# Packed attention and a channel mixer on one core: two sweeps over halves of w2's rows, in one manual order with planned side steps

## The chip, the cores and the metric

The kernel runs on one core of one Trainium2 chip. A core has TensorE (PE, matrix products into PSUM), VectorE (DVE), ScalarE (ACT), GpSimd (POOL) and SyncE (SP, which here issues every DMA). Engines run their own instructions in program order and wait for each other by semaphores. The metric is the device time of one execution in microseconds (us); lower is better.

## The reference, cut to what matters

```python
# q, k, v: (8, 8, 576, 64); p: (8, 8, 32, 64); U: (576, 32); V: (32, 576)
# w_ch1: (512, 2048); w_ch2: (2048, 512); the last four arrive as float64
def sm_attn(qq, kk, vv):
    s = scale * np.matmul(qq, kk.transpose(0, 1, 3, 2))
    s = s - np.max(s, axis=-1, keepdims=True)
    a = np.exp(s)
    a = a / (np.sum(a, axis=-1, keepdims=True) + 1e-09)
    return np.matmul(a, vv)
p_packed = sm_attn(p, k, v)
out = sm_attn(q, p_packed, p_packed)
x = out.transpose(0, 2, 1, 3).reshape(8, 576, 512)
h = x.transpose(0, 2, 1) @ U @ V
u = x + h.transpose(0, 2, 1)
ch = np.maximum(u @ w_ch1, 0.0) @ w_ch2
return (u + ch).astype(np.float32)
```

For each of 8 batches, 32 packed tokens per head attend to all 576 tokens, and all tokens then attend to the 32 packed ones. A low-rank mixing over the tokens and a two-layer perceptron follow. Since `out` is a product of attention weights (576 x 32 per head) with `p_packed`, the kernel never forms it: it multiplies `p_packed` into w1 ahead of time (the fold, giving 256 rows by 2048 columns for each batch) and mixes the attention weights instead of the tokens.

## The kernel before, in words

Products in the perceptron use three matmuls each (`mm3`): both operands are split into a rounded part (h) and a rest (l). The float64 weights are read as pairs of words and turned to float32 in chunks of 128 x 512 by `float32_of` (one ACT and four DVE instructions, L67 to L71), and then split (L123 ACT, L124 POOL).

**First stage** (L482 on, ordered by the scheduler). Over 16 units, half a batch's heads each: loads of k and v; a DVE transpose of k (L101); scores against a block diagonal of p (`a_scores`, L325, plain fp32); softmax; transposes of the weights on PE (`a_turn`, L345); packed tokens (`a_pack`, L361). Beside it all 16 chunks of w1 are converted and split, U and V are prepared (`prepare_uv`), and the folds for batches 0 to 3 are multiplied (`fold`, L384) and stored to DRAM (`wsr`). `attention(0)` runs here too.

**Main loop** (L695 on, in manual order). For each batch and each of 16 blocks kt of 128 hidden channels: `gemm1(kt)` (12 matmuls into `h_ps`, in two halves of 256 and 320 tokens), then ACT's Relu into `hh` (L641) and DVE's rest `hl` (L643), with the last 64 tokens kept in `hjh` and `hjl`; `gemm2(kt - 1)` adds 12 matmuls into four PSUM banks `o`, one for each 128 tokens. For each second batch `joint` (L671) makes the product of the kept tokens of two batches. `add_u` adds the residual. The folded weights are loaded by `load_wt` from DRAM and split by `split_wt` (L455 ACT, L456 POOL), a piece for two kt.

Side work stands at fixed places of that loop, one step each: `attention(b + 2)` as 16 closures (DVE transpose of q, scores with split operands, softmax on ACT, DVE and POOL, transposes `t_ps` L228, `m_ps`, `v_ps`), the conversion of w2's 16 tiles in batch 0, and the fold for batches 4 to 7, for which w1 is loaded and converted again (`later`, L554).

Of the kernel before, what the change touches and what calls it, by code (L numbers as in the profile page):

```python
# [15 lines left out]
DRAM = bass.MemoryType.DRAM  # L16


@with_exitstack
def packed_attention_mixer_kernel(  # L20
# [22 lines left out]

    nc = tc.nc
# [6 lines left out]
    NB = S // 32  # L51
    SM = 512
    NK = DF // P
    NU = 2 * B
    QW = 256
    scale = 1.0 / float(D) ** 0.5
    HALF = ((0, 256), (256, 320))
# [4 lines left out]

    def float32_of(x, t, raw):


        low, high = raw[:, :, 0], raw[:, :, 1]
        nc.scalar.activation(t, high.bitcast(F32), AF.Abs)  # L67
        nc.vector.tensor_single_scalar(t, t, LEAST, op=ALU.max)  # L68
        nc.vector.tensor_scalar(x, t.bitcast(I32), 3, 0x3FFFFFF8, op0=ALU.logical_shift_left, op1=ALU.bitwise_and)  # L69
        nc.vector.scalar_tensor_tensor(x, high, -0x40000000, x, op0=ALU.bitwise_and, op1=ALU.bitwise_or)  # L70
        nc.vector.scalar_tensor_tensor(x, low, 29, x, op0=ALU.logical_shift_right, op1=ALU.bitwise_or)  # L71
        return x.bitcast(F32)
# [10 lines left out]
    psT = ctx.enter_context(tc.tile_pool(name="psT", bufs=2, space=PSUM))  # L83

# [3 lines left out]
    bdq = const.tile([P, 4, P], F32, name="bdq")  # L88
    nc.gpsimd.memset(bdq, 0.0)

    wsr = [dram.tile([2 * H * NP, DF], F32, name=f"wsr{r}", tag=f"wsr{r}") for r in range(2)]
    wsc = {b: dram.tile([H * NP, DF], F32, name=f"wsc{b}", tag=f"wsc{b}") for b in range(B // 2, B)}


    def load_nat(pool, bufs, src, b, g):
        nat = pool.tile([P, NB * D], F32, name="nat", bufs=bufs)
        nc.sync.dma_start(out=nat, in_=src[b, 4 * g:4 * g + 4].rearrange("h (i c) d -> (h i) (c d)", c=NB))
        return nat

    def transposed(t, nat):  # L100
        nc.vector.transpose(  # L101
            t.rearrange("p h (i c) -> p c h i", c=NB),
            nat.rearrange("p (c h l) -> p c h l", h=2, l=32),
        )
        return t


    def weight_tiles(name):
        return [
            tuple(pipe.tile([P, DF], F32R, name=f"{name}{x}{i}", tag=f"w{x}{i}") for x in "hl") for i in range(4)  # L110
        ]

    def conv_tile(dtype):
        return pipe.tile([P, DM], dtype, name="os", bufs=3)
# [4 lines left out]
    def fold_tile(dtype):  # L119
        return pipe.tile([P, 512], dtype, name="fold", bufs=6)  # L120

    def split(x, hi, lo):
        nc.scalar.copy(hi, x)  # L123
        nc.gpsimd.tensor_tensor(lo, x, hi.bitcast(F32), op=ALU.subtract)  # L124


    uh = const.tile([P, 5, 4, R], F32R, name="uh")
    ul = const.tile([P, 5, 4, R], F32R, name="ul")
    vs = const.tile([P, S], F32R, name="vs")

    def load_uv(pool):
        bits = pool.tile([P, NB * D], F32, name="nat", bufs=3)
        ub = bits[:, :10 * R].bitcast(I32)
        nc.gpsimd.memset(ub[64:, 8 * R:], 0)
        nc.sync.dma_start(out=ub[:, :8 * R].rearrange("p (k r) -> p k r", k=4),
                          in_=U[:SM].rearrange("(k p) r -> p k r", p=P))
        nc.sync.dma_start(out=ub[:64, 8 * R:], in_=U[SM:])
        vbits = pool.tile([P, NB * D], F32, name="nat", bufs=3).bitcast(I32)
        for a in range(4):
            nc.sync.dma_start(out=vbits[32 * a:32 * a + 32], in_=V)  # L140
        return ub, vbits

    def prepare_uv(ub, vbits):
        ux = float32_of(conv_tile(I32)[:, :5 * R], conv_tile(F32)[:, :5 * R], ub.rearrange("p (x t) -> p x t", t=2))
        for (n, ks) in ((P, slice(0, 4)), (64, slice(4, 5))):
            nk = ks.stop - ks.start
            src = ux.rearrange("p (k r) -> p k r", k=5)[:n, ks].unsqueeze(2).to_broadcast([n, nk, 4, R])
            nc.vector.tensor_copy(uh[:n, ks], src)
            nc.vector.tensor_tensor(ul[:n, ks], src, uh[:n, ks].bitcast(F32), op=ALU.subtract)
        vb = vbits.rearrange("p (x t) -> p x t", t=2)  # L150
        for c0 in (0, S // 2):
            cs = slice(c0, c0 + S // 2)
            vx = float32_of(conv_tile(I32)[:, :S // 2], conv_tile(F32)[:, :S // 2], vb[:, cs])
            nc.vector.tensor_copy(vs[:, cs], vx)
            for a in (2, 3):
                as_ = slice(32 * a, 32 * a + 32)
                nc.vector.tensor_tensor(vs[as_, cs], vx[as_], vs[as_, cs].bitcast(F32), op=ALU.subtract)


    def attention(b, res):  # L160

        st = {}

        def load(g):
            st["nat", g] = load_nat(pipe, 1, q, b, g)

        def blocks():
# [18 lines left out]
        def scores(g, hf):  # L186
            hi, lo = st["q", g]
            bqh, bql = st["bq"]
            if hf == 0:
                st["e", g] = pipe.tile([P, NB, 32], F32, name="e", bufs=1)  # L190
# [215 lines left out]
    def convert_w1(c):  # L406
        x = float32_of(conv_tile(I32), conv_tile(F32), wbits.pop(c))
        if c + 2 < 16:
            wbits[c + 2] = load_w1(c + 2)
# [378 lines left out]
```

## Time and profile before

| what | value |
|---|---|
| median of the runs | 877.01 us (876.28 to 878.86, three runs) |
| the profiled execution's own time | 877.77 us |
| its span, first to last instruction | 876.0 us |
| TensorE's mean granted clock | 0.987 |
| DMA, mean over the span | 112 GB/s, 98.55 MB |
| POOL busy | 258.6 us (30%) |

The page sums each engine's busy time and follows back the chain of work that ended last. The views by window give busy times for a stretch. The timeline gives starts and lengths; lengths of matmuls are modelled and overlap, so the distance between starts is the rate. A row of a group reads: line, engine, operation, out<-in, shapes, count, then busy us and mean ns, then the engine's idle time ahead of these instructions and who ended it.

### The profile page before, as it was taken

Reading aid. Unit: us, or ns where it says so; the run is one execution under the profiler, and the core shown is the slowest. Engines: PE = TensorE matmul, PEld = TensorE weight load, DVE = VectorE, ACT = ScalarE, POOL = GpSimd, SP = SyncE. Lnnn points to the kernel's source line nnn. Section 1 sums busy time; section 2 is a strip of 40 time slices with the busy share of each in tenths; the row PEclk is TensorE's granted clock in tenths of the full one; section 3 lists DMA queues with packets and bytes.
Section 4 is the critical chain, followed back from the end, with each engine's and each line's share of the span. In section 5 each row is a group of like instructions: output and inputs, shape, how many; then the busy total and the mean of one; then the engine's idle time right before and its main releaser. Section 6 shows DMA issues by size and latency. Waiting matters only on the chain.

```text
span 876.0 us, 12670 instructions
## 1 busy us (share of the span) xinstructions
PE 827.1 (94%) x4480; PEld 708.5 (81%) x4480; DVE 518.6 (59%) x1042; ACT 374.6 (43%) x960; POOL 258.6 (30%) x230
## 2 busy tenths in 40 slices
PE   4779898889999999999999999999999999999997
PEld 2556576677879888888888888988888889889886
DVE  7999986789767875577675443443543524432220
ACT  2557676534444554456554332233332322333220
POOL 3302353545443213132323232323241313221110
PEclk9989999999999999999999999999999999999999
DMA  9769775823333444344453103010301120002001
GB/s 316 237 208 331 213 225 207 256 87 126 128 100 108 120 148 124 97 121 121 124 172 85 52 19 112 26 56 13 112 25 64 62 62 25 25 13 96 25 1 60
DMA packets 59998, 98.55 MB, mean 112 GB/s; under 512 B 12192, under 2 KB 36768, under 8 KB 59936
## 3 DMA queue, kind: packets, MB, share of 16 engines
q1 hardware_dynamic: 59936, 97.75, 35.9%
q8 instruction: 35, 0.57, 0.3%
q14 instruction: 27, 0.22, 0.1%
HBM read 71.52 MB, written 26.21 MB: 112 GB/s over the span
## 4 chain that ended last, share of the span: by engine, by line
PE 72%; DVE 18%; DMA 4%; issue 3%; ACT 3%; SPq 0%; DVEq 0%; ACTq 0%
PE o L78 15%; PE o L76 14%; PE o L77 14%; PE h_ps L76 7%; PE h_ps L77 7%; PE h_ps L78 7%; DVE kT L101 4%; DVE os L70 2%; DVE os L69 2%; DVE os L71 2%; PE w_ps L595 2%; DVE natT L101 2%; DVE os L68 2%; DMA bits<-in_moe_w_ch_dram 1%; PE t_ps L228 1%
## 5 line engine op out<-in xcount | busy, mean ns | idle before, releaser
L643 DVE SCALAR_TENSOR_TENSOR hl<-h_ps,hh 128x256 fp32r<-128x256 f32 x256 | 104.1, 418 | 180.2 <-ACT hh L641 145.0
L78 PE MATMUL o<-w2h,hl 128*128 128x512 f32 x512 | 201.8, 394 | 0.0
L76 PE MATMUL o<-w2h,hh 128*128 128x512 f32 x512 | 200.9, 392 | 0.0
L77 PE MATMUL o<-w2l,hh 128*128 128x512 f32 x512 | 200.4, 391 | 0.0
L641 ACT ACTIVATE hh<-h_ps 128x256 fp32r<-128x256 f32 x256 | 96.1, 383 | 235.0 <-PE h_ps L78 232.0
L76 PE MATMUL h_ps<-ah,fold 128*128 128x256 f32 x496 | 149.7, 302 | 7.5 <-DVE hl L643 7.1
L456 POOL TENSOR_TENSOR fold<-fold 128x512 fp32r<-128x512 f32 x62 | 81.4, 1313 | 230.7 <-ACT fold L455 225.3
L77 PE MATMUL h_ps<-al,fold 128*128 128x256 f32 x496 | 146.5, 295 | 0.0
L78 PE MATMUL h_ps<-ah,fold 128*128 128x256 f32 x496 | 146.0, 294 | 0.0
L78 PEld LDWEIGHTS o<-w2h,hl 128*128 128x128 f32 x512 | 96.1, 188 | 21.3
L77 PEld LDWEIGHTS o<-w2l,hh 128*128 128x128 f32 x512 | 96.4, 188 | 17.6
L76 PEld LDWEIGHTS o<-w2h,hh 128*128 128x128 f32 x512 | 96.3, 188 | 16.7
L76 PEld LDWEIGHTS h_ps<-ah,fold 128*128 128x128 f32 x496 | 93.7, 189 | 14.7 <-DVE hl L643 11.5
L77 PEld LDWEIGHTS h_ps<-al,fold 128*128 128x128 f32 x496 | 93.9, 189 | 2.1
L78 PEld LDWEIGHTS h_ps<-ah,fold 128*128 128x128 f32 x496 | 93.8, 189 | 0.0
L184 POOL TENSOR_TENSOR nlo<-natT,nhi 128x576 fp32r<-128x576 f32 x32 | 46.0, 1453 | 114.8 <-ACT nhi L183 114.8
L68 DVE TENSOR_SCALAR os<-os 128x512 f32<-128x512 f32 (+2 forms) x51 | 39.5, 775 | 35.4 <-ACT os L67 35.4
L325 PE MATMUL s_ps<-kT,bdp 128*128 128x288 f32 x128 | 39.7, 460 | 9.5 <-DVE bdp L316 9.3
L183 ACT CAST nhi<-natT 128x576 fp32r<-128x576 f32 x32 | 20.7, 675 | 56.3 <-DVE natT L101 53.2
L101 DVE STREAM_TRANSPOSE kT<-nat 128x1152 f32<-128x1152 f32 x16 | 37.3, 2330 | 5.8 <-DMA nat<-in_k_dram 5.7
L325 PEld LDWEIGHTS s_ps<-kT,bdp 128*128 128x128 f32 x128 | 26.4, 215 | 17.6 <-issue 9.3
L124 POOL TENSOR_TENSOR w1l<-os,w1h 128x512 fp32r<-128x512 f32 x16 | 21.2, 1328 | 62.3 <-ACT w1h L123 62.3
(145 smaller groups left out, 1419.7 us busy)
## 6 DMA issues: line engine op xcount, KB each, us to landing
bits<-in_moe_w_ch_dram SPq DMA_DIRECT2D x48, 512.0 KB, 4.3
nat<-in_k_dram SPq DMA_DIRECT2D x16, 576.0 KB, 4.9
nat<-in_q_dram SPq DMA_DIRECT2D x16, 576.0 KB, 4.5
vt<-in_v_dram SPq DMA_DIRECT2D x16, 512.0 KB, 5.5
wsr<-fold SPq DMA_DIRECT2D x32, 256.0 KB, 3.7
out_dram<-bits SPq DMA_DIRECT2D x16, 512.0 KB, 3.0
wsc<-bits SPq DMA_DIRECT2D x64, 128.0 KB, 2.2
fold<-wsc SPq DMA_DIRECT2D x32, 256.0 KB, 2.8
```

Of the source, the lines that this page charges most:

```text
L68: nc.vector.tensor_single_scalar(t, t, LEAST, op=ALU.max)
L76: nc.tensor.matmul(ps, lhsT=lh, rhs=rh, start=start, stop=False)
L77: nc.tensor.matmul(ps, lhsT=lh, rhs=rl, start=False, stop=False)
L78: nc.tensor.matmul(ps, lhsT=ll, rhs=rh, start=False, stop=stop)
L101: nc.vector.transpose(t.rearrange("p h (i c) -> p c h i", c=NB), nat.rearrange("p (c h l) -> p c h l", h=2, l=32),)
L124: nc.gpsimd.tensor_tensor(lo, x, hi.bitcast(F32), op=ALU.subtract)
L183: nc.scalar.copy(hi[:, dh], t)
L184: nc.gpsimd.tensor_tensor(lo[:, dh], t, hi[:, dh].bitcast(F32), op=ALU.subtract)
L325: nc.tensor.matmul(s_ps[:, hf, :288], lhsT=bdp[b % 2][:, 2 * g + dh], rhs=kT[:, dh, 288 * hf:288 * hf + 288], start=dh == 0, stop=dh == 1)
L456: nc.gpsimd.tensor_tensor(lo, raw, hi.bitcast(F32), op=ALU.subtract)
L641: nc.scalar.activation(hi, src, AF.Relu)
L643: nc.vector.scalar_tensor_tensor(lo, src, 0.0, hi.bitcast(F32), op0=ALU.max, op1=ALU.subtract)
```

## The change

The main loop becomes two sweeps: kt 0 to 7 for all eight batches, then kt 8 to 15. The first sweep's sums go to DRAM (`sums`, `sumj`) and are added when the second sweep's are stored; the split tokens go to DRAM as well (`asp`) and are loaded again (`reload_a`). Only half of w1 (two quarters of its columns at a time) and half of w2 are held; w2's later half is converted in the first sweep, kept in DRAM (`w2d`) and reloaded between the sweeps. w1 is converted once.

There is no first stage by itself. The whole program is in manual order. Packs, attention, folds and conversions are generators; each yields after a step and tells the PE time, the engine times, the PSUM banks and the buffers of its next one. A planner, `Chains`, keeps a clock of each engine and, after each half of `gemm1` and each tile of `gemm2`, places the steps that are ready by it, earliest due first. `until` lets its clock run until named steps are done. The loop starts after `until("attention0", "fold0_0", "w2_0")`.

Further: k and q are turned by PE transposes (`turn`: nine of 128 x 128 for each unit, with ACT and DVE copies out of PSUM) instead of DVE's L101; scores are eight fp32 matmuls with 64 rows and 32 columns for each unit, for q unsplit; the packed tokens are 20 matmuls 32 columns wide. The halves of `gemm1` are 288 tokens each, and 32 kept tokens come from each half. `mixing` takes 10 matmuls for 15. V is converted once on 128 partitions, stored to DRAM (`vd`) and loaded back four times.

```diff
+class Chains:
+    def ready(self, name):
+        c = self.left[name]
+        return (c["at"] <= self.now
+                and (c["due"] <= self.horizon or max(self.free["DVE"], self.free["ACT"]) <= self.now)
+                and all(n in self.flags or n in self.done and self.done[n] <= self.now for n in c["after"])
+                and all(t <= self.now for t in self.banks[:c["need"]])
+                and all(self.resources[r] >= c["take"].count(r) for r in c["take"]))
...
+    def place(self, pe=0.0, ops=()):
+        self.spend(pe, ops)
+        banks = went = 0
+        for _ in range(4):
+            names = [n for n in self.left if (banks == 0 or self.left[n]["need"] == 0) and self.ready(n)]
+            if not names:
+                break
+            name = min(names, key=lambda n: self.left[n]["due"])
+            banks += self.left[name]["need"]
+            self.go(name)
+            went += 1
+        return went
+    def until(self, *names):
+        while not all(n in self.flags or n in self.done and self.done[n] <= self.now for n in names):
+            if not self.place():
+                self.now += 0.1
...
+    side = Chains(6, xt=NX, xT=2, e=3, eT=2, pT=1, aT0=1, aT1=1)
+    side.slow = 1.7
...
+        nc.sync.dma_start(out=vd, in_=vx)
+        v4 = sA.tile([P, S], F32, name="v4")
         for a in range(4):
-            nc.sync.dma_start(out=vbits[32 * a:32 * a + 32], in_=V)
+            nc.sync.dma_start(out=v4[32 * a:32 * a + 32], in_=vd.rearrange("(r a) x -> r (a x)", a=P // R))
...
+    def turn(x, t, **then):
+        pairs = x.rearrange("p a x -> p (a x)")
+        for h2 in range(2):
+            t_ps = bank()
+            for a in range(4):
+                c = 4 * h2 + a
+                nc.tensor.transpose(t_ps[:, P * a:P * a + P], pairs[:, P * c:P * c + P], ident)
+            nc.scalar.copy(t[:, 2 * h2:2 * h2 + 2, HT:HS], t_ps.rearrange("p (h x) -> p h x", h=2))
+            yield step(0.45, ("ACT", 0.59), need=1, wait=False)
...
+    def scores(lT, t, g):
+        ss = [bank() for _ in range(2)]
+        for h in range(4):
+            hs = slice(32 * h, 32 * h + 32)
+            for r in range(2):
+                rs = slice(64 * r, 64 * r + 64)
+                nc.tensor.matmul(ss[r][hs, :HS], lhsT=lT[rs, g, hs], rhs=t[rs, h, HT * (1 - r):HT * (1 - r) + HS], start=True, stop=True)
+        return ss
...
+        yield step(0.75, ("DVE", 1.2), ("ACT", 1.4), need=1, take=("eT",))
...
+        for kk in range(5):
+            rows = P if kk < 4 else 64
             for h in range(4):
                 hs = slice(32 * h, 32 * h + 32)
+                rhs = vk[:, kk, h] if kk < 4 else vx[:rows, 4, D * h:D * h + D]
+                nc.tensor.matmul(p_ps[hs, :D], lhsT=eT[:rows, kk, hs], rhs=rhs, start=kk == 0, stop=kk == 4)
...
+        yield step(1.1, ("ACT", 0.35), need=1)
...
+    def fold(r, parts, fresh=(0, 1)):
...
+            for pr in range(4):
+                w_ps = bank()
+                mm3(w_ps, (lwh[:, pr], lwl[:, pr]), w1_slices(pr, c), True, True)
+                st = out_tile()
                 nc.scalar.copy(st, w_ps)
+                for b2 in batches:
+                    nc.sync.dma_start(out=wsb[2 * r + b2, c][64 * pr:64 * pr + 64], in_=st[64 * b2:64 * b2 + 64])
...
+    side.until("attention0", "fold0_0", "w2_0")
+    for i in range(2):
+        load_wt(i)
+        split_wt(i)
...
+            for hf in range(2):
+                n0, n = HS * hf, HS
...
+                side.place(0.8, [("ACT", 0.58), ("DVE", 0.6)])
...
+                mm3(self.o[t], (hh[:, ts_], hl[:, ts_]), w2t[kt], kt == self.kts[0], kt == self.kts[-1])
+                side.place(0.7)
+        def store(self):
+            for t in range(4):
+                os_ = out_tile()
...
+                if self.sw == 1:
+                    nc.vector.tensor_tensor(os_, self.o[t], self.part[:, t], op=ALU.add)
...
+    for sw in range(2):
...
+        for b in range(B):
+            if sw == 0 and b > 0:
+                side.until(f"attention{b}")
+            cur = Batch(sw, b)
...
+                if (sw, b) == (0, 0) and j == 2:
+                    side.until("fold0_1")
+                    load_wt(2)
+                if sw == 0 and b % 2 == 1 and j == 4 and b + 1 < B:
+                    side.until(f"fold{(b + 1) // 2}")
...
+                cur.gemm1(kt)
...
+                if j > 0:
+                    if (sw, b) == (0, 0):
+                        side.until(f"w2_{kt - 1}")
+                    cur.gemm2(kt - 1)
...
+                        if sw == 1 and b == 0:
+                            for k2 in range(NKS, NK):
+                                reload_w2(k2)
...
+                side.place()
```

More of the change, by code (lines that the diff above doesn't have):

```diff
@@ L19, in packed_attention_mixer_kernel, with step @@
+def step(pe, *ops, need=0, take=(), due=None, wait=True, after=()):
+    return pe, ops, need, take, due, wait, after
 @with_exitstack
@@ L100, in transposed @@
[L100 to L114, printed above, removed]
+    ppT = {}
+    ppTd = [dram.tile([P, 2 * P], F32, name=f"ppTd{b}", tag=f"ppTd{b}") for b in range(B)]
```

1062 lines of the change are left out of this document (532 added, 530 removed).

## The prediction

> **What bounds the kernel now.** I read the page first, then the windows, then TensorE's timeline. The page says what the end hangs on:
>
> ```profile
> span 876.0 us, 12670 instructions
> PE 827.1 (94%) x4480; PEld 708.5 (81%) x4480; DVE 518.6 (59%) x1042; ACT 374.6 (43%) x960; POOL 258.6 (30%) x230
> PE 72%; DVE 18%; DMA 4%; issue 3%; ACT 3%; SPq 0%; DVEq 0%; ACTq 0%
> ```
>
> TensorE (PE) holds 72% of the chain that ended last, and VectorE (DVE) 18%. The windows (columns: stretch, length, then busy us and instructions of PE, PEld, DVE, ACT, POOL; clock; DMA share; GB/s) show that these are two different kernels, one after the other:
>
> ```profile
> 0.00:160.40 160.40, 127.08 (x529) 92.79 (x530) 140.59 (x247) 94.43 (x235) 56.12 (x64) 0.95 0.79 250
> 160.40:876.00 715.60, 699.98 (x3952) 615.72 (x3950) 378.06 (x795) 280.16 (x726) 202.45 (x166) 1.00 0.27 82
> 25.00:125.00 100.00, 85.56 (x361) 63.28 (x360) 95.88 (x175) 63.36 (x166) 29.89 (x25) 0.93 0.77 240
> ```
>
> The first stage lasts 160.4 us; in its middle DVE is busy 95.88 of 100 us, and PE issues 361 matmuls there against some 550 in 100 us later, so its 85.56 us is mostly modelled overlap. After 160.4 us PE is idle for 715.6 - 700.0 = 15.6 us in all, 4.5 of them after its last matmul. So the first stage is bound by DVE, the rest by PE's stream. One step of the main loop, free of side work, from the timeline (start, length):
>
> ```profile
> 160.41 0.28 PE L76 MATMUL h_ps<-ah,wt 128*128 128x256 f32 x1
> ...
> 816.92 0.28 PE L76 MATMUL h_ps<-ah,fold 128*128 128x256 f32 x1
> ...
> 818.50 0.39 PE L76 MATMUL o<-w2h,hh 128*128 128x512 f32 x1
> 818.73 0.39 PE L77 MATMUL o<-w2l,hh 128*128 128x512 f32 x1
> ...
> 821.26 0.28 PE L76 MATMUL h_ps<-ah,fold 128*128 128x256 f32 x1
> ```
>
> Each step takes 821.26 - 816.92 = 4.34 us: 12 matmuls of gemm1 in 1.58, 12 of gemm2 at 0.23 each. Starts, not the modelled lengths, give the rate.
>
> **The main work is not changed: 629 us.** Two sweeps of 8 steps over 8 batches are again 128 steps, 128 x 4.34 = 555.5. Halves of 288 instead of 256 and 320 stream the same columns. The joint products stay 192 matmuls of 512 columns (45 us), the residuals 192 + 48 of 256 columns at 0.12 (29 us; spacing in the rows of m_ps below).
>
> **What goes: the wait of the main loop for the whole first stage.** The loop now begins when batch 0 has its attention, the first quarter of w1 is converted and folded, and w2's first tile is there. Rows for the start and the conversions:
>
> ```profile
> 0.73 0.45 SPq L296 DMA_DIRECT2D pn<-in_p_dram  x1
> 3.46 0.61 SPq L303 DMA_DIRECT2D vt<-in_v_dram  x1
> 5.74 2.34 DVE L101 STREAM_TRANSPOSE kT<-nat 128x1152 f32<-128x1152 f32 x1 [5.74 <-DMA nat<-in_k_dram]
> L68 DVE TENSOR_SCALAR os<-os 128x512 f32<-128x512 f32 x48 | 38.2, 796 | 35.4 <-ACT os L67 35.4
> L69 DVE TENSOR_SCALAR os<-os 128x512 int32<-128x512 int32 x48 | 31.6, 658 | 1.8
> L70 DVE SCALAR_TENSOR_TENSOR os<-bits,os 128x512 int32<-128x512 int32 x48 | 37.4, 779 | 1.3
> L71 DVE SCALAR_TENSOR_TENSOR os<-bits,os 128x512 int32<-128x512 int32 x48 | 35.6, 741 | 1.3
> L201 DVE TENSOR_REDUCE m<-e 128x18 f32<-128x576 f32 x16 | 12.0, 749 | 0.3
> L216 DVE STREAM_TRANSPOSE aT<-e 128x576 f32<-128x576 f32 x16 | 12.3, 771 | 10.9 <-POOL e L214 10.9
> wsr<-fold SPq DMA_DIRECT2D x32, 256.0 KB, 3.7
> fold<-wsc SPq DMA_DIRECT2D x32, 256.0 KB, 2.8
> ```
>
> A converted chunk costs DVE 0.796 + 0.658 + 0.779 + 0.741 = 2.97 us. Up to the loop DVE owes five chunks (15), two head groups of attention at about 4.2 each (two reductions at 0.749, a transpose at 0.771, the scores' transposes and smaller ones), its mixing 4, four pack units at 2, U and V 4 (estimates from the same rows by their element counts): 39 us. It can begin near 6 (first data) and ends near 45. The chain by itself, packs, scores, softmax, mixing, is of like length. The fold's store (3.7), the load of the first piece (2.8) and its split (about 2) come behind: some 8 us. First loop matmul at **55 us**. With DVE never waiting and no chain behind it, 46; with DVE at 60%, 75. V's way through DRAM costs two landings, about 6 us, beside the packs and ahead of the mixing; without that cover up to 6 us. SyncE (SP) issues about 30 loads first, 14 us at 0.45 to 0.61 each; the packs follow as these land, and the first chunk of w1 comes behind them.
>
> **What moves into the loop: PE's side work.** The rows for its price:
>
> ```profile
> 744.37 0.29 PE L76 MATMUL s_ps<-nhi,bqh 128*128 128x288 f32 x1
> 744.50 0.29 PE L77 MATMUL s_ps<-nlo,bqh 128*128 128x288 f32 x1
> ...
> 762.96 0.82 PE L228 MATMUL t_ps<-ident,aT 128*128 128x128 f32 x6
> ...
> 769.15 0.28 PE L77 MATMUL m_ps<-tl,uh 128*128 128x256 f32 x1
> 769.27 0.28 PE L78 MATMUL m_ps<-th,ul 128*128 128x256 f32 x1
> 769.48 0.38 PE L76 MATMUL m_ps<-th,uh 64*128 64x256 f32 x1
> 769.70 0.28 PE L77 MATMUL m_ps<-tl,uh 64*128 64x256 f32 x1
> 769.82 0.28 PE L78 MATMUL m_ps<-th,ul 64*128 64x256 f32 x1
> 770.03 0.38 PE L76 MATMUL h_ps<-ah,fold 128*128 128x256 f32 x1
> ...
> 114.23 2.10 PE L325 MATMUL s_ps<-kT,bdp 128*128 128x288 f32 x8
> 117.54 1.89 PE L361 MATMUL pp_ps<-vt,eT 128*128 128x256 f32 x8
> ```
>
> A transpose is (0.82 - 0.27) / 5 = 0.11 us, a 256-column matmul 0.12, a 288-column one 0.13, a 512-column one 0.23. In the loop fall: 12 pack units x 15 transposes (20 us), 14 attention groups x 9 (14), seven mixings at 10 transposes, 10 matmuls of 256 columns and 4 of 288 (20), p (1), 64 fold products x 0.69 (44): 99 us. Moved with them are their copies on ScalarE (ACT) and DVE, which stand beside PE's stream, and their loads and stores. The transposes stand for DVE's L101, 32 x 2.3 us, which go.
>
> Two kinds of matmul are new: scores as eight fp32 matmuls on tiles of 64 x 32 of the array, and the packed output as 20 on tiles 32 columns wide. Nothing in the trace runs on such tiles. The fp32 rows above show two instructions per call (L325, x8 for four calls of 288 columns in 2.1 us). With no overlap eight calls cost 4.2 us; if all overlap, one call's 0.53. For the packed output (64 columns, a quarter of L361's 256, so 0.06 per instruction) it is 2.4 or 0.6. I take the step sizes in the diff's own plan, 0.75 and 1.1, near the low ends: wherever a row exists, that plan agrees with it (0.45 for four transposes, 0.7 for three of 512 columns). In the loop: 26 x 0.75 + 12 x 1.1 = 33 us; ends 21 and 138.
>
> Leaving the full array costs too. Around the 64-row matmuls the starts stand 0.21, 0.22 and 0.21 apart where 0.12 is normal: 0.28 us an excursion. 26 scores, 12 packs, 7 mixings, 45 x 0.28: **13 us**. The Trainium skill, TensorEngine Tiling (Array Packing), section Tiling Modes, says that changing the mode drains TensorE. It speaks against this change, and the trace agrees by those 0.28 us; without it the sum would be 13 us less.
>
> **Waits in the loop.** One row now carries nearly all of them:
>
> ```profile
> PE h_ps L76 <- DVE hl L643: 9.7, 8, 2.2
> ```
>
> They fall where 16 chunks of w2 are converted. After, 11 chunks (33 us of DVE), packs 2 and 3 (8), attention 1 (12), the splits of the folds and the loop's own DVE work (12 steps at 1.2) meet between 55 and about 140 us, some 70 of 85 us. gemm2 waits for each w2 tile, the next batch for attention 1 and fold 1; PE's order is fixed, so behind a late step stands all of gemm1 and gemm2, and behind those ACT and DVE. Later sweep 0 has DVE at two thirds. The batch ends double (16 for 8), and in sweep 1 DVE alone empties four banks. I take 20 us, from 11 (as now) to 50. Stores and reloads of partial sums, w2 and the split tokens bring about 40 MB, to some 160 GB/s, below the 250 of the first stage; hidden, but for a microsecond or two where w2 is reloaded. SP's issues grow from some 330 to over 600, about 300 of 855 us at 0.5 each: no bound, but SP takes them in order, and a store that waits for its copy has the next pieces' loads behind it, for which gemm1 waits.
>
> **Sum.** 55 + 629 + 99 + 33 + 13 + 20 + 5 (the tail, now 4.5) = 854 us of span. The profiled run took 877.77 with a span of 876.0, so 856 against it; its time is 0.8 above the median of 877.01: **855**.
>
> **Rivals.**
> Tiles do not overlap as planned (chance 0.23), the case on the other side. If each call's second half waits for its first and the next call for that half, scores cost nine halves of 0.26, 2.3 us, and the packed output stays at 1.1: 26 x 1.55 = 40 more, **895**, slower. Wholly serial it is about 960. It decides from 1.6 us per score step, as 26 x 0.85 eats the 22 us. For it: no overlap shows anywhere in the trace. Against: the plan's constants fit elsewhere. The Trainium skill, TensorE: Matmul & The Clock Gate, Part 3, has tiles start about 4 ns apart, but matmuls in strict order; the first gives the forecast, the second this rival. No run here shows either.
>
> The early loop is starved (0.15): DVE and ACT fall behind the planned clocks, SP's queue holds loads behind stores that wait, and the start comes at 70 with 30 us of waits: **880**. For it: DVE at 95.88 of 100 us today. Against: the removed DVE work.
>
> The early start does not come about (0.05): the until on attention0 or on the first fold holds PE to 100 us; about 900.
>
> Better (0.07): start at 48 with 8 us of waits: 836 or less.
>
> **How the numbers follow.** The forecast has 0.50, with 838 to 872 as its own range. Measurement tells about 0.3% here, 874.4 to 879.6. Faster: 0.50 + 0.07 and a little of the starved case, 0.61. Same: 0.07. Slower: 0.32. The range runs from 830 to 898; outside stay the serial tiles, the failed start and the best half of Better.
>
> **What would show it.** The first h_ps matmul near 55 us, not 160. A score step of eight matmuls within 0.6 to 1.0 us of PE starts; 2.3 or 4.2 proves the first rival. DVE's total near 400 us instead of 518.6 (74 of L101 and 48 of 16 chunks go, since w1 is converted once). PE idle after the start about 20 us, most of it before 150 us, waiting for DVE. Wrong it would be by gaps ahead of gemm2 for w2, of gemm1 for a piece still landing, or by a hole between the sweeps.

## The result, and the profile after

| | before | after |
|---|---|---|
| median of the runs, us | 876.64 (875.63 to 878.86) | 975.76 (973.88 to 979.09) |
| ratio, 95% interval | | 1.1116 (1.1094 to 1.1137): slower |
| span of the profiled execution, us | 876.0 | 972.3 |
| first product of the main loop at, us | 160.4 | 84.9 |
| TensorE's mean granted clock | 0.987 | 0.925 |

The forecast was 855, with a range to 898. The time lies 121 us above the one and 78 above the other. The page of the changed kernel (the span; busy time by engine; PE, DVE and the granted clock in 40 slices of 24.3 us; the chain that ended last):

```profile
span 972.3 us, 15520 instructions
PE 851.4 (88%) x5452; PEld 703.8 (72%) x5452; DVE 412.9 (42%) x1122; ACT 367.6 (38%) x1065; POOL 198.0 (20%) x193
PE   4563697888999839999987999999999999999997
...
DVE  2663556433556624444477722314131332423232
...
PEclk9665788798999979999998999999999999999999
...
PE 71%; DMA 9%; DVE 8%; ACT 4%; POOL 3%; issue 3%; SPq 1%; DVEq 0%; ACTq 0%; POOLq 0%
```

DVE has become lighter, 412.9 us against 518.6, and is never full any more: its busiest slices are at 7 tenths. DMA's share of the chain went from 4% to 9%. The clock row is the new thing: 5 to 8 tenths from 24 to 195 us. The windows part the span at the loop's start and between the sweeps; then come batches 0 and 3 of sweep 0 alone (columns as before: stretch, length, busy us and instructions of PE, PEld, DVE, ACT, POOL; clock; DMA share; GB/s):

```profile
0.00:84.90 84.90, 39.63 (x374) 27.42 (x374) 42.80 (x98) 34.01 (x79) 18.42 (x26) 0.71 0.54 157
84.90:612.00 527.10, 458.63 (x3099) 364.40 (x3100) 264.89 (x670) 229.13 (x628) 139.54 (x136) 0.91 0.48 148
612.00:972.30 360.30, 353.14 (x1981) 311.96 (x1979) 105.16 (x354) 104.49 (x358) 40.02 (x31) 1.00 0.42 132
84.90:185.80 100.90, 77.18 (x458) 57.14 (x458) 56.28 (x120) 42.77 (x105) 28.13 (x25) 0.75 0.49 145
314.10:395.10 81.00, 62.42 (x433) 47.24 (x430) 36.91 (x91) 33.00 (x88) 18.76 (x18) 0.89 0.53 162
```

Sweep 1 is as the sum had it: 360.3 us at clock 1.00, with PE busy in all but 7 of them, 5 of these after its last product (64 steps, five joint products, the residuals and 24 fold products are 354 us by the prediction's prices). All of the loss lies ahead of it. The loop starts 30 us later than forecast. Sweep 0 takes 527.1 us; the forecast's span of 854, less its start (55), its tail (5) and sweep 1 as measured to its last product (355), left 439 for it, so sweep 0 is 88 too long. Those 88 us part into three:

- **Idle.** PE is idle 527.1 - 458.6 = 68.5 us, where 20 were forecast: 48 more.
- **Clock.** Cut into stretches of 0.5 us, the granted clock of sweep 0 is 1.00 in 859 and 0.50 in 176 of 1055, so the mean of 0.91 stands for about 95 us at half clock. PE is idle in 29 of these; in the other 66 it does about half the work, which makes that work some 33 us longer, an estimate from these figures. The forecast had no such term.
- **The rest**, 7 us, is left over; no run says what it is.

So 30 + 48 + 33 + 7 = 118 us, which is 972.3 - 854. This divides up PE's time; it does not say what the kernel would gain if one part alone went. That PE does half the work at half clock is seen in PE's timeline of batch 0, where products of 512 columns start 0.43 us apart (the clock is 0.50 from 95.8 to 98.3 us) and 0.23 a little later (1.00 from 99.9 to 102 us):

```profile
96.23 0.63 PE L167 MATMUL o<-w2l,hh 128*128 128x512 f32 x1
96.66 0.63 PE L168 MATMUL o<-w2h,hl 128*128 128x512 f32 x1
...
100.37 0.39 PE L168 MATMUL o<-w2h,hl 128*128 128x512 f32 x1
100.60 0.39 PE L166 MATMUL o<-w2h,hh 128*128 128x512 f32 x1
```

The first rival, tiles that do not overlap, is ruled out by the timeline of PE, once before the loop and once in it (start, length, then the shape of the tiles; x16 are the two instructions each of eight calls):

```profile
14.03 0.83 PE L395 MATMUL t_ps<-xT,pT 64*32 64x288 f32 x16
14.79 0.90 PE L470 MATMUL t_ps<-xt,eT 128*32 128x64 f32 x40
...
146.85 0.29 PE L168 MATMUL h_ps<-ah,wtl 128*128 128x288 f32 x1
147.07 0.72 PE L395 MATMUL t_ps<-xT,ppT 64*32 64x288 f32 x16
147.72 0.40 PE L166 MATMUL h_ps<-ah,wth 128*128 128x288 f32 x1
147.96 0.29 PE L167 MATMUL h_ps<-al,wth 128*128 128x288 f32 x1
148.09 0.30 PE L168 MATMUL h_ps<-ah,wtl 128*128 128x288 f32 x1
```

A score step takes 147.72 - 147.07 = 0.65 us in the loop and 0.76 before it, as the plan's 0.75 had it. The ways in and out show too: 0.22 and 0.24 us where products of this width stand 0.13 apart, so 0.20 us an excursion. Scores, packs and switches were sized rightly or a little high.

What ends the waits now? The view of waits over the whole span (engine and line, what it waited for, total us, times, longest) names many things where before it named one:

```profile
PE t_ps L166 <- ACT ev L598: 17.2, 3, 9.2
...
PE h_ps L166 <- ACT wth L620: 13.6, 1, 13.6
PE t_ps L421 <- DMA pn<-in_p_dram: 13.5, 4, 7.0
...
PE t_ps L166 <- ACT w1h L297: 13.2, 5, 4.8
```

These are the fold's copies out of PSUM (L598), the first piece of folded weights ahead of the loop (L620), p for the next batch (L421) and w1's chunks (L297). None of the four is DVE directly; PE stands where a chain that passes through several engines isn't ready.

### The profile page after: what moved, and what is told of

The parts are those of the page before. It is cut to its first block, busy times and chain, and to the rows that moved or that the text cites. A ratio compares the mean times of both kernels' runs of the same rounds, so it can differ in the third digit from the quotient of the medians.

```text
span 972.3 us, 15520 instructions
## 1 busy us (share of the span) xinstructions
PE 851.4 (88%) x5452; PEld 703.8 (72%) x5452; DVE 412.9 (42%) x1122; ACT 367.6 (38%) x1065; POOL 198.0 (20%) x193
## 4 chain that ended last, share of the span: by engine, by line
PE 71%; DMA 9%; DVE 8%; ACT 4%; POOL 3%; issue 3%; SPq 1%; DVEq 0%; ACTq 0%; POOLq 0%
PE o L166 13%; PE o L167 13%; PE o L168 13%; PE h_ps L166 7%; PE h_ps L168 6%; PE h_ps L167 6%; DMA xt<-in_k_dram 3%; PE t_ps L378 2%; PE t_ps L167 2%; PE t_ps L395 2%; PE t_ps L168 2%; PE t_ps L166 1%; DMA wsb<-ev 1%; PE t_ps L405 1%; DVE ts L229 1%
## 5 line engine op out<-in xcount | busy, mean ns | idle before, releaser
L166 PE MATMUL h_ps<-ah,wth 128*128 128x288 f32 x512 | 159.2, 311 | 17.1 <-ACT wth L620 13.6
L621 POOL TENSOR_TENSOR wtl<-raw,wth 128x512 fp32r<-128x512 f32 x64 | 83.8, 1310 | 428.2 <-ACT wth L620 415.9
L168 PE MATMUL h_ps<-ah,wtl 128*128 128x288 f32 x512 | 154.2, 301 | 1.2 <-POOL wtl L621 1.2
L167 PE MATMUL h_ps<-al,wth 128*128 128x288 f32 x512 | 154.0, 301 | 0.0
L166 PEld LDWEIGHTS h_ps<-ah,wth 128*128 128x128 f32 x512 | 99.4, 194 | 31.0 <-ACT wth L620 13.8
L167 PEld LDWEIGHTS h_ps<-al,wth 128*128 128x128 f32 x512 | 99.6, 194 | 4.0
L168 PEld LDWEIGHTS h_ps<-ah,wtl 128*128 128x128 f32 x512 | 99.1, 194 | 1.8 <-POOL wtl L621 1.8
L598 ACT COPY ev<-t_ps 128x512 f32<-128x512 f32 x68 | 39.9, 586 | 105.5 <-PE t_ps L168 77.8
L378 PE MATMUL t_ps<-ident,xt 128*128 128x128 f32 x256 | 44.5, 311 | 9.7 <-DVE aT L551 3.2
L710 ACT ACTIVATE hjh<-h_ps 128x32 fp32r<-128x32 f32 x256 | 50.1, 196 | 0.0
```

The source lines that it names most:

```text
L166: nc.tensor.matmul(ps, lhsT=lh, rhs=rh, start=start, stop=False)
L167: nc.tensor.matmul(ps, lhsT=lh, rhs=rl, start=False, stop=False)
L168: nc.tensor.matmul(ps, lhsT=ll, rhs=rh, start=False, stop=stop)
L378: nc.tensor.transpose(t_ps[:, P * a:P * a + P], pairs[:, P * c:P * c + P], ident)
L598: nc.scalar.copy(st, w_ps)
L621: nc.gpsimd.tensor_tensor(lo, raw, hi.bitcast(F32), op=ALU.subtract)
```

## The experiments

Four theories. **Queue:** SP issues every DMA in order, and a DMA stands behind others that wait or have yet to be issued. **Planner's figures:** the constants by which `Chains` orders the steps are too short. **Chains:** side work comes as chains of dependent steps across engines, and PE's fixed order stops the main products wherever a step is late, though no engine is full. **Clock:** the half clock comes from idle time, and costs time of its own. Where the first expectations number the theories, 1 is the queue, 2 DVE with the planner's figures, 3 the chains as planned. Ratios below are to the kernel before, with 95% intervals.

### The queue: e1 and e2

```diff
# e1_late_raw: the next piece's load a half step later
-                    if i + 2 < len(pieces):
-                        load_wt(i + 2)
+                if j % 2 == 1 and i > 0 and i + 2 < len(pieces):
+                    load_wt(i + 2)
# e2_act_stores: the fold's 128 stores issued by ACT
-                    nc.sync.dma_start(out=wsb[2 * r + b2, c][64 * pr:64 * pr + 64], in_=st[64 * b2:64 * b2 + 64])
+                    nc.scalar.dma_start(out=wsb[2 * r + b2, c][64 * pr:64 * pr + 64], in_=st[64 * b2:64 * b2 + 64])
```

> The reload of a folded piece (raw, one buffer) is issued one kt later, when GpSimd has read the buffer; nothing else moves. Theory 1 (SyncE's one queue is held by DMAs that wait, so the side work's loads land late and TensorE stands behind them): SyncE's waits for GpSimd in the first sweep, 122 us, go nearly to nothing, and the time falls by 20 to 40 us, to 935-955. Theory 2 (the plan's engine times are too small, DVE's conversions above all) and theory 3 (the plan's own chain of attention, with its idle time, sets the first sweep): within 6 us of 976.

> The fold's 128 stores go out from ScalarE's queue, right behind ScalarE's own copy, instead of SyncE's. Theory 1: SyncE's 42 us of waiting for these copies go from its queue, 5 to 20 us faster. Against it stands ScalarE's time to issue 128 DMAs at about 0.4 us, 50 us in all; theories 2 and 3 expect no gain, 0 to 15 us slower.

e1: 974.82 us, ratio 1.1095 (1.1079 to 1.1112). SP's largest wait halved, in the view of waits of SP's queue (total us, times, longest), of the changed kernel and then of e1:

```profile
SPq L615 <- POOL wtl L621: 194.7, 48, 10.0
```

```profile
SPq L615 <- POOL wtl L621: 97.5, 24, 8.2
```

But the waiting only moved. Summed over all its rows, that view counts 643 us of waits in the changed kernel and 642 in e1: other DMAs of the queue wait in this one's place. The time is the same within its interval: halving the largest wait changed nothing, and with the sum unchanged e1 doesn't clear the queue. e2: 992.69 us, 1.1293 (1.123 to 1.1356), slower by 17, a little more than any theory allowed. The long gaps at the fold's copies became many short ones (e2's view of waits),

```profile
PE t_ps L166 <- ACT ev L598: 14.0, 16, 3.2
```

while ACT now issues two stores after each copy before it can make the next one, which takes it from 1.1 to 2.9 us a pair in e2's timeline from 357 to 370 us. So e2 buys one delay with another, and the queue stays open; the section on the order comes back to it.

### The planner's figures: e3 and e4

```diff
# e3_consts: DVE and POOL steps at their measured lengths
-            yield step(0, ("DVE", 1.4))
+            yield step(0, ("DVE", 1.57))
...
-                yield step(0, ("ACT", 0.67), ("DVE", 0.9), due=items[i + 1][1])
+                yield step(0, ("ACT", 0.67), ("DVE", 1.6), due=items[i + 1][1])
...
# e4_dma: the landing of a load
-                t = self.free[engine] + 2.2
+                t = self.free[engine] + 5.0
```

> The plan's step sizes for a converted chunk become the measured ones (1.6 and 1.57 us on DVE for 0.9 and 1.4, 0.86 on GpSimd for 0.78); only the order of instructions can change. Theory 2: steps are placed when they can run, batch 0 falls from 101 us to about 85, in all 15 to 30 us faster. Theory 3: the order hardly matters, the plan by its own clock grows from 868 to 886 us, so 0 to 15 us slower. Theory 1: no change beyond 8 us.

> The planner's clock lets a load land 2.2 us after its issue; here 5.0 us (the pn load of batch 1 took 4.3 us from issue to landing and PE stood 7.0 us before it). Theory 'the plan's landing time is too short': the 7.0 us gap near 25 us and the like go, the time falls by 10 to 25 us, to 950 to 966. Theory 'the plan's own chain sets the end': the plan with the later landings ends 14 us later by its own clock (882 against 868), so the time rises by 0 to 15 us, to 976 to 991.

e3: 979.11 us, 1.1141 (1.1122 to 1.1159). e4: 972.09 us, 1.1056 (1.1009 to 1.1102). Batch 3 of sweep 0 went from 81.0 to 92.2 us in e3 and to 75.3 in e4, and the others made up for most of it. In e3 batch 0 fell only from 100.9 to 97 us, where the theory of the planner's figures had 85; neither theory's number for e4 was met. Truer figures alone make little difference.

### What the chains weigh: e5, e10, e11 and e8

Three kernels leave one kind of side work out each: e5 the four DVE instructions of each converted chunk, e10 the attention of batches 1 to 7, e11 the folds of batches 2 to 7.

```diff
# e5_noconv, in float32_1 and float32_2
+        if x.shape[-1] != 512:
+            nc.scalar.activation(t, high.bitcast(F32), AF.Abs)
...
+            return
+        nc.scalar.activation(x.bitcast(F32), high.bitcast(F32), AF.Abs)
...
+        if x.shape[-1] == 512:
+            return x.bitcast(F32)
# e10_noatt
-        add_attention(b)
+        res[b] = res[0]
...
-                side.until(f"attention{b}")
# e11_nofold
-        src = wsb[b, 2 * sw + cc // 512][:, cc % 512:cc % 512 + QW]
+        src = wsb[b % 2, 2 * sw + cc // 512][:, cc % 512:cc % 512 + QW]
...
-        side.add(f"fold{r}", line(0, 2 * r - 1, 3), fold(r, [(0, (0, 1)), (1, (0, 1))]),
-                 (*(f"packs{2 * r + i}{g}" for i in range(2) for g in range(2)), f"fold{r - 1}"))
```

Where a step that is left out stood as a condition, the two larger cuts put another in its place: in e10 batch 1 waits for the last tile of w2's earlier half and w2's later half for a pack, in e11 w1's later half no longer waits for the last fold.

> Leaves out the four DVE instructions of every converted chunk of w1 and w2 (ScalarE's first instruction writes the chunk instead), 32 x 3.17 = 101 us of DVE's 413; the order stays. Theory 2: the first sweep and the start are starved by DVE; at least 50 us faster, start near 65 us, batch 0 near 70. Theories 1 and 3: DVE had room; 10 to 30 us faster, and the batches after the first are as long as before.

> Leaves out the attention of batches 1 to 7 (loads of q, scores, mixing; these batches use batch 0's result); the packs and all folds stay. By the step lengths of the plan this takes some 46 us from PE (7 x 6.5) and 4 us of mode switches. Theory 'the attention chain, batch by batch, is what sweep 0 waits for': most of the 68 us of idle time in sweep 0 and of its 32 us at half clock goes too, sweep 0 falls from 527 to 400 to 430 us and the time by 95 to 125 us, to 850 to 880. Theory 'the folds and the conversions set the waits': only the work goes, the time falls by 45 to 60 us, to 915 to 930.

> Leaves out the folds of batches 2 to 7, in both sweeps (these batches read those of batches 0 and 1); packs and attention stay. This takes 48 steps of 0.7 us from PE, 34 us, half of it in each sweep. Theory 'the folds are due in bursts, and sweep 0 waits for them': the gaps near 222 and 364 us and the time of the long fourth batch go, sweep 0 falls by 45 to 60 us and the time by 60 to 75, to 900 to 915. Theory 'the attention chain sets the waits': only the work goes, the time falls by 30 to 42 us, to 934 to 946.

| kernel | us | ratio | PE work and switches gone (expected) | gone beyond that |
|---|---|---|---|---|
| e5_noconv | 942.89 | 1.0733 (1.0717 to 1.0749) | 0 | 33 |
| e10_noatt | 880.95 | 1.0045 (1.002 to 1.007) | 50 | 45 |
| e11_nofold | 922.82 | 1.0519 (1.0498 to 1.054) | 34 | 19 |

The work and switches that are gone are figures of the plan, not measured. Sweep 0 of each, by the windows of e5, e10 and e11:

```profile
78.40:580.40 502.00, 451.85 (x3099) 359.02 (x3100) 186.90 (x566) 228.96 (x628) 136.37 (x136) 0.93 0.50 155
```

```profile
86.20:519.20 433.00, 391.00 (x2581) 320.47 (x2582) 181.48 (x488) 182.90 (x530) 85.37 (x80) 0.94 0.48 142
```

```profile
86.40:579.20 492.80, 435.30 (x3026) 348.70 (x3027) 261.89 (x658) 211.80 (x592) 139.76 (x136) 0.92 0.46 145
```

e5 gives PE exactly the same work, 3,099 products, and takes 264.9 - 186.9 = 78 us from DVE in the sweep; the sweep gets 25 us shorter and the start 6.5 earlier. Were DVE the bound, 78 us less of it would show as far more; were it without effect, nothing would. The 33 us in all stand just above the 10 to 30 of the theories in which DVE had room, and well below the other's 50. e10 takes the most beyond its own work: idle falls from 68.5 to 42.0 us, and the clock rises to 0.94. Its time lies just outside what the attention theory gave (850 to 880), far from the other's 915 to 930. e11 lies between its two. So the 118 us have no single source: with each of the three kinds of chain some idle time and some half clock go, beyond its work, with attention the most. No run leaves out two kinds, so the three figures can't be added up. Even with attention of seven batches left out the kernel is no faster than before.

A fourth run removes a wait of the start: V is loaded four times from the input instead of going through DRAM.

```diff
# e8_vdirect
-        nc.sync.dma_start(out=vd, in_=vx)
-        v4 = sA.tile([P, S], F32, name="v4")
...
+            nc.sync.dma_start(out=vb[32 * a:32 * a + 32].rearrange("p x t -> p (x t)"), in_=V)
```

> V is read four times from the input and converted on 128 partitions, instead of once on fewer rows and through DRAM. Theory 'V's way through DRAM lies beside other work': within 5 us of 975.8. Theory 'V's way holds the first scores': the first h_ps starts 5 us or more before 84.9 and the time falls by as much.

978.77 us, 1.1141 (1.1112 to 1.1169), 3 from the changed kernel, first `h_ps` at 86.3. V's way is covered, as the prediction had it, to within the DVE time that e8 adds by its own plan (3.4 us for 1.1).

### The order: e6, e13 and e14

```diff
# e6_foldsplit: half of the next fold due now, half a batch later
-                    side.until(f"fold{(b + 1) // 2}")
+                    side.until(f"fold{b + 1}_0")
+                if sw == 0 and b % 2 == 0 and b > 0 and j == 0:
+                    side.until(f"fold{b // 2}")
# e13_horizon: steps may run further ahead of their due points
-                side.horizon = line(sw, b, kt) + 6
+                side.horizon = line(sw, b, kt) + 10
# e14_early_piece, on top of e13
-    side.until("attention0", "fold0_0", "w2_0")
-    for i in range(2):
-        load_wt(i)
-        split_wt(i)
+    side.until("fold0_0")
+    load_wt(0)
+    side.until("attention0", "w2_0")
+    split_wt(0)
+    load_wt(1)
+    split_wt(1)
```

The aim of e6 is one stop, seen in the timeline of SP, ACT and PE of the changed kernel (last, in brackets, the idle time and what ended it):

```profile
350.02 0.59 ACT L598 COPY ev<-t_ps 128x512 f32<-128x512 f32 x1 [1.60 <-PE t_ps L168]
350.27 1.18 SPq L353 DMA_DIRECT2D xt<-in_k_dram  x1
...
358.56 0.98 SPq L367 DMA_DIRECT2D xt<-in_v_dram  x2
360.21 10.41 SPq L600 DMA_DIRECT2D wsb<-ev  x16
363.55 0.58 ACT L598 COPY ev<-t_ps 128x512 f32<-128x512 f32 x1 [9.72 <-DMA wsb<-ev]
364.19 0.79 PE L166 MATMUL t_ps<-w1h,lwh 128*128 128x512 f32 x1 [9.23 <-ACT ev L598]
```

`until("fold2")` runs a fold's eight products one after the other; each needs a copy into one of three `ev` buffers, and each buffer its two stores. The first copy is done at 350.61 us, but SP first issues 16 loads of k and v for packs, from 350.27 to 359.54, and the fold's 16 stores only from 360.21 on; the fourth copy waits for the first of these. The gap of 7.1 us in batch 1 has the same picture, with 16 loads issued from 208.97 and the stores from 218.04. So SP's order is the last link in these two stops, 16 of the 68.5 us. In e2, where the stores had left that queue, no stop at these copies was longer than 3.2 us. No run put the stores ahead of the loads.

> The order's due points for w2's folds are split: a main batch waits for half of the next fold only, and the second half is due one batch later. Nothing is computed differently. Theory 'the planner's due points force bursts': the burst of eight products near 360 us goes, with most of the 9.2 us and 7.1 us gaps of PE; the fourth batch of sweep 0 falls from 81 to about 66 us, and the time by 5 to 20 us, to 956 to 971. Theory 'the clock gate': only what the gaps took with them, under 5 us. Theory 'the side chain is late in any order': what is gained in batch 3 comes back in batches 4 and 5, and the time is within 3 us of 975.8.

> One number of the planner: side steps may go ahead of their due point by 10 lines of the main loop instead of 6. Same work, another order; by the planner's own clock the end comes 16.5 us earlier (851.9 against 868.4), all of it in batches 3 to 7 of sweep 0. Theory 'the order itself sets the waits in sweep 0, as the planner's clock counts them': the time falls by 10 to 22 us, to 954 to 966. Theory 'the chip runs late against the planner's clock wherever the chains are put': within 6 us of 975.8.

> On top of e13: the first piece of the folded weights is loaded as soon as its fold is stored (the last of its four stores is issued near 66 us), instead of after batch 0's mixing, where it stood in SP's queue behind the two spills of the tokens and landed 6.1 us after its issue at 78.1. Theory 'the last 8 us before the loop are this load and its place in the queue': the first h_ps starts near 79 instead of 86 and the time falls by 4 to 8 us, to 952 to 956. Theory 'what is won at the start is lost in batch 0, which waits for its conversions and for attention 1 in any case': first h_ps near 79, the time within 3 us of 960.

e6: 983.5 us, 1.1186 (1.1154 to 1.1218). Batch 3 shrank from 81.0 to 74.3 us, but batches 1 and 2 grew from 67.1 and 61.2 to 77.0 and 73.1: splitting the due point moved the loss to earlier batches and added 8 us. None of the three theories had a rise. e13: 960.04 us, 1.0929 (1.0908 to 1.095), 16 less than the changed kernel, by one number that changes nothing but the order. Its windows:

```profile
86.20:587.10 500.90, 452.64 (x3098) 361.48 (x3099) 262.34 (x670) 229.57 (x628) 141.37 (x136) 0.93 0.51 156
587.10:958.10 371.00, 356.25 (x1981) 314.45 (x1979) 105.64 (x354) 104.47 (x358) 40.04 (x31) 0.99 0.40 129
```

Sweep 0 gains 26 us, and 11 come back in sweep 1, whose first batch takes 59.3 us for 48.4, with a stop of 7.2 us at a fold's copy and a clock of 0.94. Idle time in sweep 0 is 48 us now, and the clock 0.93. e14 looks at the start. The chain before the loop, in the changed kernel's view of the chain that ended last (start, length, what; only part of it):

```profile
1.74 4.18 DMA xt<-in_k_dram
...
13.13 5.08 DMA xt<-in_q_dram
...
20.63 5.75 DMA xt<-in_k_dram
26.44 3.82 DMA vd<-vx
...
59.82 1.37 DVE wd L234
...
61.94 0.63 ACT w1h L297
62.64 1.28 POOL w1l L298
63.96 0.79 PE t_ps L167
...
73.76 3.94 POOL al L556 x4
77.72 0.33 SPq L567
78.09 6.15 DMA raw<-wsb
84.26 0.63 ACT wth L620
```

For 30 us it runs through loads of 4 to 6 us each, then from engine to engine in steps of 0.5 to 1.5 us, and at its end through the first piece's load, which waits in SP's queue behind the mixing's results though its fold was done near 68. e14 issues it earlier: 953.91 us, 1.0852 (1.0832 to 1.0872), first `h_ps` at 77.8. Of 8.4 us won at the start, 6.1 reach the end; that is what the place of this one load in SP's order was worth.

### The clock: e7, e9 and e12

Wherever the planner's clock finds nothing for PE, 847 steps of 0.1 us in all, these add products of a constant tile; the rest of the order stays.

```diff
# e9_warm256 (in e7_warm behind the next line; e12_warm_one takes its tile once a wait)
+                self.fill()
                 self.now += 0.1
...
# e7_warm: two products of 128 columns, in a new PSUM tile each time
+        for _ in range(2):
+            nc.tensor.matmul(w_ps[:, :P], lhsT=warm, rhs=warm, start=True, stop=True)
# e9_warm256: one of 256 columns, in a new PSUM tile each time
# e12_warm_one: one of 256 columns, all of one wait in one PSUM tile
```

> The order is unchanged; wherever the planner's clock finds nothing to put on PE, two products of a constant tile (128 columns) are added per 0.1 us of planned idle time. Theory 'half clock after idle time costs some 43 us (11 before the loop, 32 in sweep 0)': the mean granted clock rises from 0.925 to over 0.97 and the time falls by 20 to 43 us, to 933 to 956. Theory 'half clock costs little, because PE waits for others in those stretches': the clock rises and the time moves by less than 5 us. Against both: where PE is late in fact, the added products delay it, by up to 10 us.

> As e7_warm, in another dose: per 0.1 us of the planner's idle time one product of 256 columns (some 0.11 us at the rate of the main products) instead of two of 128 columns, which took 0.16 to 0.28 us each, so that 847 steps add some 91 us of PE work to places where PE stood idle 110 us. Theory 'half clock is due to idle time, and costs some 43 us': the mean granted clock rises to over 0.96 and the time falls by 15 to 40 us, to 935 to 960. Theory 'half clock comes with the small products of the side chains, idle or not': the clock stays under 0.94 and the time rises by 0 to 40 us, to 976 to 1016, as far as the added products stand where PE was late.

> As e9_warm256, but all added products of one wait of the planner go into one PSUM tile, so that none waits for the one before (in e9 each took 0.22 to 0.58 us from start to start, and the engine waited 501 times for its own last product). 847 products of 256 columns at some 0.11 us: 91 us of work, laid where PE stood idle 110 us. Theory 'half clock follows idle time and costs some 43 us': the mean granted clock rises to over 0.96, the time falls by 10 to 40 us, to 935 to 965. Theory 'half clock comes with the small products and the waits of the side chains, and products put into the planner's idle time do not lift it': clock under 0.94, time 975 to 1010.

e7 and e9 missed their dose: 1355.58 us, 1.5444 (1.5389 to 1.5498), and 1268.42 us, 1.4474 (1.4415 to 1.4533), clock 0.832 and 0.854. Their additions were several times dearer than meant: in e9, from 194.97 us on, 18 of them take 11.46 us, 0.64 each for some 0.11. In e9 a product that took a new tile waited for PE's own last one (the tile's view: lengths min/median/max; then the idle time it ended):

```profile
L219 PE MATMUL h_ps<-warm x558: 276/582/583, 131.3 to 810.9; 128*128 128x256 f32 x186
...
  PE h_ps L219: 166.1, 501
```

e7's window from 165 to 245 us is worth a look all the same, since PE counts as busy 74.8 of 80 us there, and yet the granted clock is one half throughout (16 additions of 128 columns take 5.89 us there, from 170.41 on, so they start 0.37 us apart, and their modelled lengths fill the time between):

```profile
165.00:245.00 80.00, 74.83 (x256) 55.11 (x257) 12.77 (x26) 7.82 (x16) 6.26 (x5) 0.50 0.06 17
```

e12 got the dose right. A row of its timeline, with 35 additions that take 4.43 us, some 0.12 each, and then its windows:

```profile
235.76 4.43 PE L221 MATMUL h_ps<-warm 128*128 128x256 f32 x35
```

```profile
0.00:95.50 95.50, 67.39 (x663) 59.95 (x663) 42.17 (x98) 33.30 (x79) 18.25 (x27) 0.88 0.48 140
95.50:640.90 545.40, 503.32 (x3657) 422.95 (x3658) 264.41 (x670) 230.31 (x628) 139.84 (x136) 0.95 0.47 143
```

Before the loop the clock rises from 0.71 to 0.88, in sweep 0 from 0.91 to 0.95; the mean is 0.963. So products put into idle time do lift the clock. But the time is 1000.71 us, 1.1395 (1.1371 to 1.1419), 25 more. 847 x 0.12 = 102 us were added; PE's busy time up to the end of sweep 0 rose by only 72.5 (67.4 + 503.3 against 39.6 + 458.6), so the other work got some 29 us cheaper; and PE's idle time fell from 113.7 to 70.2 us, by 43, less than half of what was added. The planner's idle time is not where PE is idle in fact: where a wait on the chip is shorter than planned, the additions delay it. Of the two theories' numbers the first had the clock right and the second the time. What the kernel would take at full clock with nothing added, no run shows.

## Why the prediction was wrong, point by point

**The start, 55 us forecast, 84.9 measured: +30.** The step that failed is the start by DVE's debt of 39 us, which "can begin near 6 (first data) and ends near 45", with a chain that by itself "is of like length". DVE's debt was nearly right (42.80 us up to 84.9), but it has this work spread over twice the time: in the chain that ended last, DVE holds 15 of these 85 us and DMA 32. That chain goes through loads up to 30 us, which I took to lie beside the work, then through all engines, then through a piece load of 6.15 us where the before kernel's median of 2.8 stood in the sum. PE works there at a mean clock of 0.71, which makes its work some 11 us longer by the reckoning of sweep 0. The rival with a start "at 70 with 30 us of waits" was nearer; both its numbers were still too kind.

**The waits in the loop, 20 us forecast, 68.5 measured: +48.** The reasoning "Later sweep 0 has DVE at two thirds" took the busiest engine's share as the measure of waiting. DVE is busy 50% of sweep 0 (264.89 of 527.10), its total of 412.9 near the forecast's 400, and PE waits all the same. e5, e10 and e11 show that each kind of side work brings its waits, beyond its work, and e13 that the order of the steps alone is worth 16 us; in the two long stops at the folds, 16 us, SP's order is the last link. What the prediction should have asked is how late the last step of each chain comes, handover by handover, for every `until`, since behind a late step in PE's fixed order stands the main work. The before kernel had placed one step at a time two batches ahead; this planner lets steps go 6 lines ahead of their due points, and further only while its clocks of DVE and ACT are free.

**The clock: no term, where the reckoning gives 33 us in sweep 0 and 11 (among the 30) at the start.** I used durations from a loop at clock 1.00 and never asked what becomes of them when the same work is thinned out with idle time. The trace of before held the warning: its first stage, where PE issued least, stood at 0.95, its loop at 1.00. So, perhaps, did the diff: by `side.slow = 1.7` the planner takes each PE step ahead of the loop as 1.7 times as long; why, it doesn't say. The Trainium skill, TensorE: Matmul & The Clock Gate, Part 1, says that the array's clock is halved by default, and that about 3.4 us of sustained activity frees it while an idle window of like length throttles it again. e12 agrees in direction (0.71 to 0.88 before the loop); e7's row shows that PE's busy share in the profile doesn't tell the clock (94% busy at 0.50).

**Right.** The tiles: 0.65 and 0.76 us a score step in the rows shown, so the rival with the largest chance was dead. The switches: 0.20 us against 0.28. The main work: sweep 1 holds at 1.00. V's way through DRAM. DVE's total. SP's queue was a danger in another form than the one I named: gemm1's waits inside the loop for a piece still to come are 1.2 us, by the view of waits, but the fold's stores stood behind loads for packs.

**The rivals.** "The early loop is starved" had the right mechanism, with a chance of 0.15 and a price of 25 us, where its two items, the start and the waits, cost 78, and 118 with the clock and the rest. It was priced as DVE and ACT lagging behind the planned clocks and loads standing in SP's queue; but much of the idle time is in the plan. By the planner's own clock, which the program sums up as it lays out the order, PE finds nothing to do for 84.7 us (28.9 ahead of the loop, which it starts at 69.8, and 55.8 in sweep 0), and the program ends at 868, to which come 29 us of residual products that it doesn't count (240 x 0.12): 897 without a single delay on the chip. So the plan itself, which could be read ahead of any run, had the start 15 us behind the forecast's 55 and 36 us more of idle time than its 20. That is arithmetic, not a measurement, and it tracks the chip only in part: it had e13's gain right (16.5 against 16), and for e6 a gain of 5.6 where 8 were lost.

**Open.** How the 68.5 us of idle time divide between steps planned late and steps late against the plan, since e12 shows that the two don't fall in the same places; how much of them a better order in SP's queue alone would take away; and whether any order brings sweep 0 near 439 us. The best order tried, e14, stays at 953.91 us, 8.5% behind the kernel before.

## What to carry to other kernels

When side work moves from a stage of its own into a busy engine's fixed order, price it by the length of its chains against the time until they are due, not by the busy shares of the engines: here all shares fell, and PE's idle time in sweep 0 was 68.5 us where 20 were forecast. If the order comes from a planner, read first how much idle time its own clock holds. Follow the DMAs' issue order too: a store behind 16 loads held PE for 9.2 us. Add a term for TensorE's clock wherever its work gets thinner; here the half clock made its work some 44 us longer, by the estimate above. To tell work from waiting, leave one kind of side work out at a time and subtract its own work, as in e5, e10 and e11.

## What the hardware showed that was not expected

- Eight fp32 calls on tiles of 64 x 32 take 0.65 us together, by the rows at 147.07 and 147.72, although each still issues two instructions.
- The granted clock can stay at one half for 80 us while PE counts as busy 94% of the time (e7).
- Products into newly taken PSUM tiles waited for PE's own last product 501 times, 166.1 us in all (e9), where products into one tile followed each other 0.12 us apart (e12).
- The same DVE instruction, on 128 x 512 words, took from 415 to 1401 ns in one execution, as the view of that line shows:

```profile
L229 DVE TENSOR_SCALAR ts<-ts x32: 415/1038/1401, 25.2 to 541.8; 128x512 f32<-128x512 f32 x32
```
